# Gated linear attention and a feed-forward block on one core: reading finished sums behind all products of their tile, block sums on VectorE, and an activation of one exp and two tanh terms

## The chip, the cores and the metric

The kernel runs on 1 core of one Trainium2 chip. The metric is the device time of one execution in microseconds; lower is better. Before the change the runs shown took 700.88 us (median of 3, 696.11 to 701.51).

## The reference

Two stages follow each other. The first is a recurrent attention over 4 batches, 8 heads, 768 positions and a head size of 48; the second is a feed-forward block of 3072 tokens, model width 384 and inner width 2048.

```python
f = 1.0 / (1.0 + np.exp(-f_logit))
for t in range(S):
    state = f[:, :, t, :, None] * state + np.einsum('bhd,bhe->bhde', k[:, :, t], v[:, :, t])
    y[:, :, t] = np.einsum('bhd,bhde->bhe', q[:, :, t], state)
x = y.transpose(0, 2, 1, 3).reshape(B * S, H * D)
h = x @ w_in
sp = np.maximum(h, 0.0) + np.log1p(np.exp(-np.abs(h)))   # softplus
g = h * erf(sp)
out = g @ w_out
```

All arrays are float32.

## The kernel before, in words

**Attention** goes by chunks of 128 positions, 24 in all (`g`), in four stages each. `stage_d` (L353) multiplies the logarithms of the decays with a triangle (`ps_d`), ScalarE takes two exponentials (`dp`, `kd`, L365, L368), VectorE scales q into `qd` (L375), and GpSimd scales k into `kd` (L379; VectorE for the first three chunks). `stage_t` (L383) transposes both on TensorE and copies them out (`qT` by ScalarE, `kT` by ScalarE or, from chunk 9, by VectorE). `stage_s` (L401) makes the scores, masks them on VectorE (`A`, L421) and moves the state on: `Sn` by VectorE (L448), `Mbd` by GpSimd (L451). `stage_y` (L455) makes the output, which ScalarE copies into `xT` (L464).

**The feed-forward block** goes by blocks of 256 tokens (two chunks), 12 in all. `hidden` (L510) makes a group of 4 x 128 inner columns: 12 matmuls of 256 columns into the PSUM tile `hps`, which ScalarE (blocks 0 to 2, L527) or VectorE (blocks 3 to 11, L529) copies to SBUF as `h`. There are 48 groups. `activate` (L469) then replaces `h` by h * erf(softplus(h)), approximated: ScalarE makes e = sigmoid(h + b) (L155) and three terms x = tanh(k h + a) (L158), VectorE multiplies each into e, (x + b) * e (L163), ScalarE takes tanh(c e) (L490), VectorE multiplies with h (L493). `activate` is a generator of steps; `act_step` (L499) advances the groups in work, starts a new one when the youngest has done `LEAD` = 6 steps, and the main loop calls it at chosen slots.

**The output product** of a block is `project` (L621), a Strassen-like scheme of seven products of quarter blocks in place of eight, for which `sum_h` (L568) makes four sums of blocks of h per group (`a21 - ...`, each 128 x 256, on GpSimd, L550) and `sum_w` (L552) the sums of the weights, once, in the place `wT` where block 0's h had been. Block 0 is multiplied plainly (`project_first`, L594) for that reason. `project` holds two PSUM tiles of two banks each, out of the same pool of two as `hps`: the first, `ops[0]`, has the products 1, 2 and 6, the second, `ops[1]`, has 5, 7, 3 and 4. Two matmuls of 192 columns per product and group make 56 matmuls per block. Before the change the finished sums are read while the block's other products are still being made: product 1 is finished first and copied by ScalarE (L666), then come 2 and 6, then VectorE adds these (L658), then 5 and 7, then VectorE again, then 3 and 4, and VectorE a last time, before the block's DMA to DRAM (L589).

**The order** is written out by hand. The main loop (L836) runs 12 passes, `it`. Passes 0 to 2 make the hidden groups of blocks 0 to 3 and `project_first`; passes 3 to 10 each run `project(it - 2)` (56 slots) and then the hidden groups of block `it + 1` (48 slots); pass 11 runs the last three projects. A slot is one matmul of these generators. In the gaps between slots the loop places the attention stages of the block after next, by the list `at`, about 11 slots apart, act steps (from pass 3 at every fourth slot), steps of block sums, and `prepare` (L335), which takes Exp and Ln of a block's decays on ScalarE right behind a `stage_y`. Each engine takes its instructions strictly in the order in which this loop writes them, and a PSUM tile is handed over as a whole: an instruction that writes to a tile waits for the reads of that tile which stand ahead of it in the program. ScalarE's functions lie in tables; `use_exp_ln` (L321) loads the set with Exp and Ln, and the other functions load theirs.

The launch first rounds the weights (float64 words to float32) in `round_piece` (L272), seven VectorE operations per piece, 16 pieces; that fills VectorE until about 100 us.

Of the kernel before, what the change touches and what calls it, by code (L numbers as in the profile page):

```python
# [40 lines left out]
FP32 = mybir.dt.float32  # L42
# [9 lines left out]
SERF_C = 0.12675436  # L52
SERF_B = 0.20603738
SERF_KAB = (
    (0.50210557, -1.37006942, 1.36582221),
    (0.49818342, -0.11437819, 5.22837536),
    (0.83937711, -2.99136281, 5.68346943),
# [13 lines left out]
P = 128  # L71
# [3 lines left out]
def kernel(  # L75
# [40 lines left out]
    serf_bias = fixed("serf_bias", [P, 1 + len(SERF_KAB)])  # L116
    flag = fixed("flag", [P, 1], I32)
    for i, a in enumerate([SERF_B] + [a for _, a, _ in SERF_KAB]):
        nc.vector.memset(serf_bias[:, i : i + 1], a)
# [34 lines left out]
    def sigmoid(dst, h):  # L154
        nc.scalar.activation(out=dst[:], in_=h, func=AF.Sigmoid, bias=serf_bias[:, 0:1])  # L155

    def term(dst, h, i):
        nc.scalar.activation(  # L158
            out=dst[:], in_=h, func=AF.Tanh, bias=serf_bias[:, 1 + i : 2 + i], scale=SERF_KAB[i][0]
        )  # L160
# [171 lines left out]
    def other_set():  # L332
        sets[0] = 0
# [19 lines left out]
    def stage_d(g):  # L353
# [8 lines left out]
        use_exp_ln()  # L362
# [16 lines left out]
        (nc.vector if g < FIRST else nc.gpsimd).tensor_tensor(  # L379
# [21 lines left out]
    def stage_s(g):  # L401
# [39 lines left out]
        for r in range(2):  # L441
            total = Tall[rows(r), g, :].unsqueeze(2).broadcast_to((D, HP, D))
            if c == 0:
                nc.vector.tensor_tensor(
                    out=new[rows(r), :, r, :], in0=dS[rows(r)], in1=total, op=ALU.mult
                )
                continue
            nc.vector.tensor_tensor(  # L448
                out=Sn[rows(r)], in0=dS[rows(r)], in1=old[rows(r), :, r, :], op=ALU.add
            )  # L450
            nc.gpsimd.tensor_tensor(  # L451
                out=new[rows(r), :, r, :], in0=Sn[rows(r)], in1=total, op=ALU.mult
            )
# [15 lines left out]
    def activate(gr):  # L469
# [4 lines left out]
        other_set()  # L474
        sigmoid(e, h)
# [3 lines left out]
        for i in range(n + 2):  # L479
            if i < n:  # L480
                xs[i] = xpool.tile([P, FG * TB], FP32, name="x", tag="x")
                other_set()
                term(xs[i], h, i)
            if i >= 2:
                times(e, xs.pop(i - 2), i - 2)
            yield
        for _ in range(n):
            yield
        other_set()
        nc.scalar.activation(out=e[:], in_=e[:], func=AF.Tanh, scale=SERF_C)  # L490
        yield
# [18 lines left out]
    def hidden(blk, gi):  # L510
# [4 lines left out]
        for j in range(FG):  # L515
            ft = gi * FG + j
            assert ft * n_pieces // n_ft in rounded
            for kt in range(n_k):
# [6 lines left out]
                if j == FG - 1 and kt == n_k - 1:  # L525
                    if blk < 3:
                        nc.scalar.copy(out=gr["h"], in_=hps[:])  # L527
                    else:
                        nc.vector.tensor_copy(out=gr["h"], in_=hps[:])  # L529
                    acts.append(activate(gr))  # L530
# [18 lines left out]
    def add(out, x, y, op=ALU.add):  # L549
        nc.gpsimd.tensor_tensor(out=out, in0=x, in1=y, op=op)  # L550

    def sum_w(gi):  # L552
# [4 lines left out]
        add(t[:, 0], b12, b11, ALU.subtract)  # L557
        yield
        add(t[:, 1], b22, t[:, 0], ALU.subtract)
        yield  # L560
        add(t[:, 2], b22, b12, ALU.subtract)
        yield
        add(t[:, 3], b21, t[:, 1], ALU.subtract)
# [57 lines left out]
    def project(blk):  # L621
# [43 lines left out]
        yield from products((2, 3), (1,))  # L665
        nc.scalar.copy(out=o[:, 3, :], in_=place[1])  # L666
        yield from products((2, 3), (2, 6))

        plus(o[:, 0:5:4, :], o[:, 3:4, :].broadcast_to((P, 2, DH)), pair(2))
        yield from products((2, 3), (5, 7))  # L670

        plus(o[:, 5:7, :], o[:, 4:5, :].broadcast_to((P, 2, DH)), pair(5))
        plus(o[:, 3, :], o[:, 5, :], place[7])
        yield from products((2, 3), (3, 4))
        plus(o[:, 1:3, :], o[:, 5:7, :], pair(3))
# [41 lines left out]
    with tc.manual_schedule():  # L717
# [118 lines left out]
        for it in range(n_blocks):  # L836
            gen, n = slots(it)
            if it == 0:
                todo = [(stage_d, 3), (stage_t, 3), (stage_d, 4), (stage_s, 3), (stage_t, 4), (stage_y, 3),
                        (stage_d, 5), (stage_s, 4), (stage_t, 5), (stage_y, 4)] + stages(2)[4:]  # L840
                at = [3, 7, 11, 14, 18, 21, 36, 44, 60, 74, 78, 82, 86, 92]
# [6 lines left out]
            for s, _ in enumerate(gen):  # L848
# [26 lines left out]
                else:  # L875
                    step = s % 4 == 2
# [21 lines left out]
    def general():  # L898
# [132 lines left out]
        def second(b, r0):  # L1031
            for gi in range(n_g):
# [12 lines left out]
                sigmoid(e, h)  # L1045
# [62 lines left out]
```

## Time and profile before

| what | value |
|---|---|
| median of the runs shown | 700.88 us |
| the profiled execution's own time | 701.82 us |
| its span, first to last instruction | 700.1 us |
| TensorE busy (matmul) | 627.1 us, 90% |
| VectorE busy | 479.6 us, 69% |
| ScalarE busy | 429.0 us, 61% |
| GpSimd busy | 278.9 us, 40% |
| granted TensorE clock, mean of full speed | 0.964 |

The busy times are sums over the whole span; which engine holds up which is read from the stretches and the waits. In the rows, PE is TensorE, PEld its weight loads, DVE VectorE, ACT ScalarE, POOL GpSimd, SP the queue that issues the DMAs. A float32 matmul leaves two records, so 56 matmuls show as 112. A number behind a name such as `ops_1915` in the program's order is that of the tile, so that two tiles of one name can be told apart.

### The profile page before, as it was taken

The numbers are of one execution on the slowest core, as the hardware profiler recorded it, in microseconds if no ns is written. First come the engines' busy times: TensorE is split into PE (matmuls) and PEld (weight loads), VectorE is DVE, ScalarE is ACT, GpSimd is POOL, SyncE is SP. The second block draws the span as 40 slices with busy tenths as digits, with TensorE's granted clock in tenths as the row PEclk, the third lists the DMA queues.
The fourth block names the chain that finished last, engine by engine and source line by source line (L and its number), as shares of the span: only waits on it lengthen the run. The fifth ranks groups of instructions, "written<-read, shape, count | busy, mean of one in ns | idle before, by whom it ended". The sixth has DMA issues, their size and how long they took to land.

```text
span 700.1 us, 11595 instructions
## 1 busy us (share of the span) xinstructions
PE 627.1 (90%) x4727; PEld 545.9 (78%) x4727; DVE 479.6 (69%) x508; ACT 429.0 (61%) x474; POOL 278.9 (40%) x253
## 2 busy tenths in 40 slices
PE   7979889999795998699899799789899999899995
PEld 6858667787485888588789688678888988789895
DVE  4799996388947676477496485656857866568751
ACT  5348358587756966838676747755686645637530
POOL 0110000123967423183183170335427560724990
PEclk9999999999898999899999899989999999999999
DMA  9998611312010301211031031030110000000000
GB/s 198 257 246 239 168 35 35 57 35 46 11 46 12 68 13 26 56 33 24 13 81 23 13 68 30 17 68 12 24 36 1 1 24 1 1 22 1 23 23 27
DMA packets 120635, 37.04 MB, mean 53 GB/s; under 512 B 112384, under 2 KB 115456, under 8 KB 120576
## 3 DMA queue, kind: packets, MB, share of 16 engines
q1 hardware_dynamic: 118496, 35.84, 22.0%
q8 instruction: 39, 0.64, 0.4%
q10 hardware_dynamic: 2080, 0.39, 0.3%
q14 instruction: 20, 0.16, 0.1%
HBM read 31.46 MB, written 4.72 MB: 52 GB/s over the span
## 4 chain that ended last, share of the span: by engine, by line
PE 64%; DVE 15%; ACT 10%; issue 4%; DMA 3%; POOL 2%; SPq 0%; ACTq 0%; DVEq 0%; POOLq 0%
PE hps L519 27%; PE ops L650 24%; PE y L149 4%; DVE e L163 3%; PE sc L407 3%; ACT x L158 2%; PE ps_d L361 2%; DVE scratch L658 2%; PE ps_t L389 1%; PE ops L605 1%; DVE A L421 1%; ACT e L155 1%; ACT L325 1%; DMA Hg<-in_moe_w_in_dram 1%; DVE Hg L308 1%
## 5 line engine op out<-in xcount | busy, mean ns | idle before, releaser
L519 PE MATMUL hps<-xT,w_in_sb 128*128 128x256 f32 x1152 | 262.8, 384 | 0.0
L519 PEld LDWEIGHTS hps<-xT,w_in_sb 128*128 128x128 f32 x1152 | 217.0, 191 | 33.6 <-issue 3.4
L163 DVE SCALAR_TENSOR_TENSOR e<-x,e 128x1024 f32<-128x1024 f32 x144 | 204.4, 1419 | 25.1 <-ACT x L158 22.3
L158 ACT ACTIVATE x<-Hg,serf_bias 128x1024 f32<-128x1024 f32 x132 | 146.8, 1136 | 0.1
L379 POOL TENSOR_TENSOR kd<-kn,kd 128x384 f32<-128x384 f32 x21 | 22.6, 1077 | 241.1 <-ACT kd L368 182.1
L650 PE MATMUL ops<-w_out_sb,Hg 128*128 128x192 f32 x352 | 78.9, 339 | 17.6 <-ACT scratch L666 13.6
L155 ACT ACTIVATE e<-Hg,serf_bias 128x1024 f32<-128x1024 f32 x44 | 50.6, 1149 | 62.9 <-DVE Hg L493 60.2
L650 PE MATMUL ops<-wT,Hg 128*128 128x192 f32 x352 | 88.6, 334 | 0.0
L650 PEld LDWEIGHTS ops<-w_out_sb,Hg 128*128 128x128 f32 x352 | 61.1, 194 | 24.9 <-ACT scratch L666 16.8
L550 POOL TENSOR_TENSOR scratch<-Hg 128x256 f32<-128x256 f32 x40 | 52.5, 1312 | 66.5 <-PE ops L650 55.2
L650 PE MATMUL ops<-wT,scratch 128*128 128x192 f32 x320 | 77.3, 334 | 0.1
L529 DVE COPY Hg<-hps 128x1024 f32<-128x1024 f32 x36 | 44.0, 1223 | 39.2 <-PE hps L519 39.0
L493 DVE TENSOR_TENSOR Hg<-Hg,e 128x1024 f32<-128x1024 f32 x44 | 64.1, 1456 | 7.6 <-ACT e L490 7.3
L650 PEld LDWEIGHTS ops<-wT,Hg 128*128 128x128 f32 x352 | 63.5, 195 | 3.3 <-issue 2.0
L650 PE MATMUL ops<-w_out_sb,scratch 128*128 128x192 f32 x160 | 42.7, 350 | 25.4 <-DVE scratch L658 25.4
L451 POOL TENSOR_TENSOR Mbd<-Sn,Tall 48x192 f32<-48x192 f32 x32 | 28.5, 892 | 86.8 <-DVE Sn L448 85.6
L658 DVE TENSOR_TENSOR scratch<-scratch,ops 128x384 f32<-128x384 f32 (+1 forms) x44 | 22.1, 502 | 56.6 <-PE ops L650 34.8
L650 PEld LDWEIGHTS ops<-wT,scratch 128*128 128x128 f32 x320 | 57.6, 195 | 0.6 <-POOL scratch L550 0.6
L490 ACT ACTIVATE e<-e 128x1024 f32<-128x1024 f32 x48 | 50.2, 1045 | 6.2 <-DVE e L163 6.2
L464 ACT COPY xT<-y 128x384 f32<-128x384 f32 x24 | 11.5, 478 | 69.3 <-PE y L149 69.3
L375 DVE TENSOR_TENSOR qd<-qn,dp 128x384 f32<-128x384 f32 x24 | 14.2, 590 | 55.4 <-ACT dp L365 55.1
L650 PEld LDWEIGHTS ops<-w_out_sb,scratch 128*128 128x128 f32 x160 | 29.3, 203 | 28.3 <-DVE scratch L658 28.3
(111 smaller groups left out, 876.9 us busy)
## 6 DMA issues: line engine op xcount, KB each, us to landing
lt<-in_f_logit_dram SPq DMA_DIRECT2D x24, 192.0 KB, 3.3
qn<-in_q_dram SPq DMA_DIRECT2D x24, 192.0 KB, 3.7
out_dram<-scratch SPq DMA_DIRECT2D x12, 384.0 KB, 2.8
kn<-in_k_dram SPq DMA_DIRECT2D x23, 192.0 KB, 3.8
vt<-in_v_dram SPq DMA_DIRECT2D x23, 192.0 KB, 2.8
w_out_sb<-in_moe_w_in_dram SPq DMA_DIRECT2D x4, 768.0 KB, 6.1
Hg<-in_moe_w_in_dram SPq DMA_DIRECT2D x4, 768.0 KB, 7.8
Hg<-in_moe_w_out_dram SPq DMA_DIRECT2D x4, 768.0 KB, 6.6
```

The lines of the kernel that those rows point to most:

```text
L149: nc.tensor.matmul(y[M * i : M * (i + 1), kt, :], lhsT=terms[n][0], rhs=terms[n][1], start=(n == 0), stop=(n == len(terms) - 1), skip_grou ...
L155: nc.scalar.activation(out=dst[:], in_=h, func=AF.Sigmoid, bias=serf_bias[:, 0:1])
L158: nc.scalar.activation(out=dst[:], in_=h, func=AF.Tanh, bias=serf_bias[:, 1 + i : 2 + i], scale=SERF_KAB[i][0])
L163: nc.vector.scalar_tensor_tensor(out=e[:], in0=x[:], scalar=SERF_KAB[i][2], in1=e[:], op0=ALU.add, op1=ALU.mult)
L451: nc.gpsimd.tensor_tensor(out=new[rows(r), :, r, :], in0=Sn[rows(r)], in1=total, op=ALU.mult)
L490: nc.scalar.activation(out=e[:], in_=e[:], func=AF.Tanh, scale=SERF_C)
L493: nc.vector.tensor_tensor(out=h, in0=h, in1=e[:], op=ALU.mult)
L519: nc.tensor.matmul(hps[:, j, :], lhsT=w_in_sb[:, kt, ft * P : (ft + 1) * P], rhs=xTs[blk][:, kt, :], start=(kt == 0), stop=(kt == n_k - 1),)
L529: nc.vector.tensor_copy(out=gr["h"], in_=hps[:])
L550: nc.gpsimd.tensor_tensor(out=out, in0=x, in1=y, op=op)
L650: nc.tensor.matmul(place[n], lhsT=x[:, j, :], rhs=y, start=(gi == 0 and j == 0 and n in first), stop=(gi == n_g - 1 and j == 1), skip_grou ...
L658: nc.vector.tensor_tensor(out=out, in0=x, in1=y, op=ALU.add)
```

## The change

Five edits, in the order of the diff below.

1. The approximation of the activation has one exp and two tanh terms in place of a sigmoid and three. Per group ScalarE does four operations (exp, two tanh, the outer tanh) in place of five, VectorE three in place of four. Exp counts as usable in whichever table set is loaded: `use_exp_ln()` is no longer called in `stage_d`, and `other_set()` no longer ahead of e.
2. `kd` (all chunks) and `Mbd` are made by VectorE.
3. All hidden groups are copied from PSUM by ScalarE.
4. The block sums of h are made by VectorE; those of the weights stay on GpSimd.
5. In `project`, products 1, 2 and 6 of the last two groups are issued together, then the copy and the first addition; products 5, 7, 3 and 4 follow together, then the other three additions.

The slots of a few attention stages in pass 0, the steps of `activate` and the slots at which the loop calls it from pass 3 on (2 and 6 of every 9) move as well. Lines of the changed kernel are up to 11 lower: L666 is L657, L658 is L649, L163 is L160, L493 is L487, L550 is L541, L519 is L513.

```diff
-SERF_C = 0.12675436
-SERF_B = 0.20603738
+SERF_C = 1.41272172
 SERF_KAB = (
-    (0.50210557, -1.37006942, 1.36582221),
-    (0.49818342, -0.11437819, 5.22837536),
-    (0.83937711, -2.99136281, 5.68346943),
+    (-0.49563134, 0.05678801, 1.02373814),
+    (0.48999436, -1.29296666, 1.39467856),
 )
...
-    def sigmoid(dst, h):
-        nc.scalar.activation(out=dst[:], in_=h, func=AF.Sigmoid, bias=serf_bias[:, 0:1])
+    def exp(dst, h):
+        nc.scalar.activation(out=dst[:], in_=h, func=AF.Exp)
...
         nc.tensor.matmul(ps, lhsT=tri[:], rhs=lts[blk][:, j, :], start=True, stop=True)
-        use_exp_ln()
...
-        (nc.vector if g < FIRST else nc.gpsimd).tensor_tensor(
+        nc.vector.tensor_tensor(
             out=kd, in0=kns[g % NQ][:].rearrange("t (h d) -> t h d", d=D), in1=kd, op=ALU.mult
...
-            nc.gpsimd.tensor_tensor(
+            nc.vector.tensor_tensor(
                 out=new[rows(r), :, r, :], in0=Sn[rows(r)], in1=total, op=ALU.mult
...
-        other_set()
-        sigmoid(e, h)
+        exp(e, h)
         yield
         n = len(SERF_KAB)
         xs = {}
-        for i in range(n + 2):
-            if i < n:
-                xs[i] = xpool.tile([P, FG * TB], FP32, name="x", tag="x")
-                other_set()
-                term(xs[i], h, i)
-            if i >= 2:
-                times(e, xs.pop(i - 2), i - 2)
+        for i in range(n):
+            xs[i] = xpool.tile([P, FG * TB], FP32, name="x", tag="x")
+            other_set()
+            term(xs[i], h, i)
             yield
-        for _ in range(n):
+        for i in range(n):
+            times(e, xs[i], i)
+            yield
+        for _ in range(3):
             yield
         other_set()
         nc.scalar.activation(out=e[:], in_=e[:], func=AF.Tanh, scale=SERF_C)
         yield
-        yield
...
                 if j == FG - 1 and kt == n_k - 1:
-                    if blk < 3:
-                        nc.scalar.copy(out=gr["h"], in_=hps[:])
-                    else:
-                        nc.vector.tensor_copy(out=gr["h"], in_=hps[:])
+                    nc.scalar.copy(out=gr["h"], in_=hps[:])
...
-    def add(out, x, y, op=ALU.add):
-        nc.gpsimd.tensor_tensor(out=out, in0=x, in1=y, op=op)
+    def add(out, x, y, op=ALU.add, engine=nc.vector):
+        engine.tensor_tensor(out=out, in0=x, in1=y, op=op)
...
-        yield from products((2, 3), (1,))
+        yield from products((2, 3), (1, 2, 6))
         nc.scalar.copy(out=o[:, 3, :], in_=place[1])
-        yield from products((2, 3), (2, 6))
 
         plus(o[:, 0:5:4, :], o[:, 3:4, :].broadcast_to((P, 2, DH)), pair(2))
-        yield from products((2, 3), (5, 7))
+        yield from products((2, 3), (5, 7, 3, 4))
 
         plus(o[:, 5:7, :], o[:, 4:5, :].broadcast_to((P, 2, DH)), pair(5))
+        plus(o[:, 1:3, :], o[:, 5:7, :], pair(3))
         plus(o[:, 3, :], o[:, 5, :], place[7])
-        yield from products((2, 3), (3, 4))
-        plus(o[:, 1:3, :], o[:, 5:7, :], pair(3))
         store(blk)
...
-                at = [3, 7, 11, 14, 18, 21, 36, 44, 60, 74, 78, 82, 86, 92]
+                at = [3, 9, 12, 15, 20, 23, 36, 44, 60, 74, 78, 82, 86, 92]
...
-                    step = s % 4 == 2
+                    step = s % 9 in (2, 6)
```

The first place at which the order moves is TensorE's queue in the second half of a project (block 2 before, block 3 in the change, both in the steady passes). Before, a wait for ScalarE stands between product 1 and products 2 and 6, and a wait for VectorE between products 5, 7 and 3, 4 of the same tiles:

```order
L650 MATMUL ops_1915<-w_out_sb_61,Hg_112 128x192 x4
L650 MATMUL ops_1915<-w_out_sb_61,Hg_112 128x192 [waits Activation_49]
L650 MATMUL ops_1915<-wT_113,scratch_114 128x192
L650 MATMUL ops_1915<-w_out_sb_61,Hg_112 128x192
...
L650 MATMUL ops_1916<-wT_113,Hg_112 128x192
L650 MATMUL ops_1916<-w_out_sb_61,scratch_114 128x192 [waits DVE_49]
L361 MATMUL ps_d_2074<-lt_1746,tri_59 128x384 [waits DMAHW1_49,PE_49,Activation_49]
L650 MATMUL ops_1916<-wT_113,Hg_112 128x192
```

In the changed kernel the same half runs through with no such wait; the wait that is left stands at the next hidden group, which takes over the first tile:

```order
L641 MATMUL ops_2208<-w_out_sb_61,Hg_110 128x192
L641 MATMUL ops_2208<-wT_111,scratch_112 128x192
L641 MATMUL ops_2209<-wT_111,scratch_112 128x192
L641 MATMUL ops_2209<-wT_111,Hg_110 128x192
...
L358 MATMUL ps_d_2374<-lt_2036,tri_59 128x384 [waits DMAHW2_49,DVE_49,Activation_49]
L641 MATMUL ops_2209<-wT_111,Hg_110 128x192
...
L641 MATMUL ops_2209<-wT_111,Hg_110 128x192
L513 MATMUL hps_2400<-xT_1975,w_in_sb_60 128x256 [waits DVE_49]
```

The two waits inside the project are gone from TensorE's queue, and the reads of the first tile now have all of products 5, 7, 3 and 4 before `hps` needs the place.

The second place is ScalarE's queue in the same half: the copy of product 1 (L666, L657) against the block's `prepare` (L342 and L343, L339 and L340). Before, the copy stands ahead of the attention output and of `prepare`:

```order
L490 ACTIVATE e_2257<-e_2257 128x1024 [waits DVE_49]
L158 ACTIVATE x_2370<-Hg_112,serf_bias_62 128x1024 [waits Activation_49]
L666 COPY scratch_114<-ops_2267 128x192 [waits DMAHW4_49,PE_49]
L464 COPY xT_2382<-y_2383 128x3x128 [waits PE_49]
L325 ACT_TABLE_LOAD
L342 ACTIVATE lt_2091<-lt_2091 128x768 [waits DMAHW3_49,DMAHW2_49,DVE_49]
L343 ACTIVATE lt_2091<-lt_2091 128x768 [waits Activation_49]
```

In the changed kernel it stands behind them and behind a second table load:

```order
L460 COPY xT_2317<-y_2318 128x3x128 [waits PE_49]
L322 ACT_TABLE_LOAD
L339 ACTIVATE lt_2036<-lt_2036 128x768 [waits DMAHW3_49,DMAHW2_49,DVE_49]
L340 ACTIVATE lt_2036<-lt_2036 128x768 [waits Activation_49]
L155 ACT_TABLE_LOAD
L155 ACTIVATE x_2356<-Hg_110,serf_bias_62 128x1024
L657 COPY scratch_112<-ops_2208 128x192 [waits DMAHW4_49,PE_49]
```

The copy has moved behind five more ScalarE instructions. Over the whole queue ScalarE's table loads go from 61 to 20.

The third place is VectorE's queue in that project of the changed kernel, where a group's four block sums (L541) now stand among the attention's and the activation's work:

```order
L417 TENSOR_TENSOR A_2250<-sc_2241,tri_59 128x1024 [waits PE_49]
L444 TENSOR_TENSOR Sn_2261<-dS_2252,Mbd1_108 48x192 [waits PE_49]
...
L447 TENSOR_TENSOR Mbd0_107<-Sn_2261,Tall_109 48x4x48 [waits DVE_49]
L541 TENSOR_TENSOR scratch_112<-Hg_110 128x256 [waits PE_49]
L541 TENSOR_TENSOR scratch_112<-scratch_112,Hg_110 128x256 [waits DVE_49]
L541 TENSOR_TENSOR scratch_112<-Hg_110,scratch_112 128x256 [waits DVE_49,PE_49]
L541 TENSOR_TENSOR Hg_110<-Hg_110 128x2x128
L160 SCALAR_TENSOR_TENSOR e_2236<-x_2267,e_2236 128x1024 [waits Activation_49]
L395 COPY kT_2298<-ps_t_2292 128x512 [waits PE_49]
```

These sums and `Mbd` were GpSimd's before, which had nothing else in this stretch; here what follows them on VectorE waits behind them.

## Rows read from the trace of the kernel before

**Rows 1.** The page, part 1: busy time of each engine, its share, its instructions.

```profile
PE 627.1 (90%) x4727; PEld 545.9 (78%) x4727; DVE 479.6 (69%) x508; ACT 429.0 (61%) x474; POOL 278.9 (40%) x253
```

**Rows 2.** Busy time by stretch: length, five engines' busy time, clock, DMA share, GB/s.

```profile
0.00:90.10 90.10, 75.81 (x720) 63.18 (x720) 75.63 (x120) 46.57 (x67) 9.99 (x19) 0.98 0.85 215
90.10:141.80 51.70, 48.65 (x404) 40.09 (x405) 32.86 (x42) 33.25 (x42) 6.01 (x6) 0.97 0.23 43
141.80:257.80 116.00, 102.39 (x727) 81.36 (x726) 85.67 (x75) 83.82 (x87) 64.67 (x54) 0.94 0.17 35
257.80:541.30 283.50, 256.56 (x1958) 227.91 (x1957) 184.55 (x180) 191.51 (x202) 117.66 (x104) 0.95 0.16 32
488.30:541.30 53.00, 49.88 (x406) 44.45 (x405) 37.81 (x36) 40.84 (x43) 25.65 (x22) 1.00 0.09 20
541.30:693.90 152.60, 143.68 (x924) 133.40 (x922) 100.40 (x94) 73.88 (x77) 80.60 (x71) 1.00 0.03 11
```

**Rows 3.** Who waited for whom on TensorE: total us, times, longest.

```profile
PE ops L650 <- DVE scratch L658: 26.4, 11, 5.8
PE ops L650 <- ACT scratch L666: 13.6, 11, 3.0
PE ops L605 <- DVE wT L493: 5.2, 1, 5.2
```

**Rows 4.** Timeline of one project, 268 to 292 us: start, length, instruction, idle before.

```profile
273.63 0.75 PE L650 MATMUL ops<-w_out_sb,Hg 128*128 128x192 f32 x2 [1.98 <-ACT scratch L666]
278.62 0.48 ACT L464 COPY xT<-y 128x384 f32<-128x384 f32 x1 [3.99 <-PE y L149]
279.12 1.28 ACT L325 ACT_TABLE_LOAD   x1
280.41 0.84 ACT L342 ACTIVATE lt<-lt 128x768 f32<-128x768 f32 x1
...
283.44 1.06 ACT L490 ACTIVATE e<-e 128x1024 f32<-128x1024 f32 x1
...
286.81 0.94 DVE L658 TENSOR_TENSOR scratch<-scratch,ops 128x384 f32<-128x384 f32 x2
287.80 1.01 PE L650 MATMUL ops<-w_out_sb,scratch 128*128 128x192 f32 x2 [5.79 <-DVE scratch L658]
```

**Rows 5.** Groups by line and shape: busy us, mean ns, idle before and what ended it.

```profile
L163 DVE SCALAR_TENSOR_TENSOR e<-x,e 128x1024 f32<-128x1024 f32 x144 | 204.4, 1419 | 25.1 <-ACT x L158 22.3
L493 DVE TENSOR_TENSOR Hg<-Hg,e 128x1024 f32<-128x1024 f32 x44 | 64.1, 1456 | 7.6 <-ACT e L490 7.3
L529 DVE COPY Hg<-hps 128x1024 f32<-128x1024 f32 x36 | 44.0, 1223 | 39.2 <-PE hps L519 39.0
...
L658 DVE TENSOR_TENSOR scratch<-scratch,ops 128x384 f32<-128x384 f32 x33 | 18.2, 551 | 56.2 <-PE ops L650 34.8 <-ACT xT L464 19.3 <-ACT x L158 1.5
...
L527 ACT COPY Hg<-hps 128x1024 f32<-128x1024 f32 x8 | 8.1, 1013 | 5.0 <-PE hps L519 4.9
...
L658 DVE TENSOR_TENSOR scratch<-scratch,ops 128x192 f32<-128x192 f32 x11 | 3.9, 354 | 0.4
```

**Rows 6.** VectorE and GpSimd by time: one operation alone, and beside a GpSimd operation.

```profile
150.97 1.21 DVE L163 SCALAR_TENSOR_TENSOR e<-x,e 128x1024 f32<-128x1024 f32 x1
...
181.44 2.03 DVE L163 SCALAR_TENSOR_TENSOR e<-x,e 128x1024 f32<-128x1024 f32 x1
...
182.35 1.98 POOL L550 TENSOR_TENSOR wT<-w_out_sb 128x384 f32<-128x384 f32 x1
```

**Rows 7.** The chain that ended last, in order of time: start, length, what.

```profile
612.52 20.72 PE hps L519 x96
...
650.55 13.28 PE ops L650 x80
...
693.81 0.55 DVE scratch L658
```

**Rows 8.** Who waited for whom on ScalarE: total us, times, longest.

```profile
ACT e L155 <- DVE Hg L493: 60.2, 26, 7.3
```

More of the change, by code (lines that the diff above doesn't have):

```diff
@@ L115 @@
     w_out_sb = fixed("w_out_sb", [P, n_ft, d_model])
-    serf_bias = fixed("serf_bias", [P, 1 + len(SERF_KAB)])
+    serf_bias = fixed("serf_bias", [P, len(SERF_KAB)])
     flag = fixed("flag", [P, 1], I32)
-    for i, a in enumerate([SERF_B] + [a for _, a, _ in SERF_KAB]):
+    for i, a in enumerate(a for _, a, _ in SERF_KAB):
         nc.vector.memset(serf_bias[:, i : i + 1], a)
@@ L152, in y_matmuls @@
                         )
-    def sigmoid(dst, h):
-        nc.scalar.activation(out=dst[:], in_=h, func=AF.Sigmoid, bias=serf_bias[:, 0:1])
+    def exp(dst, h):
+        nc.scalar.activation(out=dst[:], in_=h, func=AF.Exp)
     def term(dst, h, i):
         nc.scalar.activation(
-            out=dst[:], in_=h, func=AF.Tanh, bias=serf_bias[:, 1 + i : 2 + i], scale=SERF_KAB[i][0]
+            out=dst[:], in_=h, func=AF.Tanh, bias=serf_bias[:, i : i + 1], scale=SERF_KAB[i][0]
         )
@@ L556, in sum_w @@
         t = w_sums(gi)
-        add(t[:, 0], b12, b11, ALU.subtract)
+        add(t[:, 0], b12, b11, ALU.subtract, nc.gpsimd)
         yield
-        add(t[:, 1], b22, t[:, 0], ALU.subtract)
+        add(t[:, 1], b22, t[:, 0], ALU.subtract, nc.gpsimd)
         yield
-        add(t[:, 2], b22, b12, ALU.subtract)
+        add(t[:, 2], b22, b12, ALU.subtract, nc.gpsimd)
         yield
-        add(t[:, 3], b21, t[:, 1], ALU.subtract)
+        add(t[:, 3], b21, t[:, 1], ALU.subtract, nc.gpsimd)
     def blocks(h):
@@ L1044, in second @@
                     nc.vector.tensor_copy(out=gs[gi][:, j, :], in_=hps[:, 0:TB])
-                sigmoid(e, h)
+                exp(e, h)
                 for i in range(len(SERF_KAB)):
```

## Prediction

> **What bounds the kernel now.** Start with the busy times on the page: TensorE works in 90% of the span, VectorE in 69%, ScalarE in 61% [rows 1]. So the end is set by TensorE's work plus the time in which TensorE stands, and the question is where it stands. The busy times by stretch answer that. Between 257.8 and 541.3 us lie five like passes (4 to 8, each with one project, four hidden groups and two attention chunks); TensorE is busy 256.56 of 283.50 us there. The last of the five is the fastest, 53.00 us with 49.88 busy at clock 1.00; the mean clock of the five is 0.95 [rows 2]. A pass without waits is thus near 49.9 us of TensorE, and the mean pass takes 56.7. The view of who waited for whom names the cause: 26.4 us for VectorE's additions L658 and 13.6 us for ScalarE's copy L666, each 11 times, once per project [rows 3]. Both are reads of a PSUM tile to which TensorE goes on writing. The timeline of one project shows how: after 1.98 us for the copy, TensorE waits 5.79 us more, because VectorE's addition stands behind ScalarE's xT copy, a table load, Exp, Ln, a second load and a tanh; the product behind each wait is shown with 0.75 and 1.01 us, where 80 records back to back take 13.28 us, 0.33 per product of two records [rows 4, 7]. So a wait costs twice: the wait, and work at the lower of the two clock levels behind it.
>
> **Term 1, the passes from 257.8 us on.** With products 1, 2, 6 together and 5, 7, 3, 4 together, no matmul writes to a tile once its reads have begun; in the changed order both waits are gone from TensorE's queue. TensorE's idle time is 283.50 - 256.56 = 26.9 us in the five passes and 152.60 - 143.68 = 8.9 us from there to the last product, together 35.9. Slow clock: five passes at 49.88 would be 249.4 us busy, and they were 256.56, so 7.2 more. Sum 43.0 us, nearly all of it behind these two waits, and I take it all as gone; what is late next comes in term 5.
>
> **Term 2, 141.8 to 257.8 us** (pass 2 with the plain product of block 0, and the first project). TensorE idles 116.00 - 102.39 = 13.6 us here, and the clock of 0.94 allows up to 0.06 x 116 = 7.0 more [rows 2]. One wait is for the activation of block 0 (5.2 us for L493) [rows 3]. VectorE is slow there because GpSimd works beside it: an operation of 1.21 us alone takes 2.03 beside one of GpSimd's [rows 6], and GpSimd is busy 64.7 of the 116 us. After the change GpSimd keeps only the 16 sums of weights, at 1.98 us 32 us, and a group needs 3 x 1.21 us of VectorE in place of 4 operations at 1.42 to 1.46 [rows 5]. Each act step brings a finished group nearer, too: 10 steps in place of 12. So the group for which TensorE waited is ready earlier. Ends: 6 us if only the project's own waits and a little go, 20.6 if all. I take 14, since GpSimd's weight sums still stand beside VectorE for a third of the stretch.
>
> **Term 3, the start to 141.8 us.** VectorE rounds weights, 75.6 of the first 90.1 us [rows 2]. Added to it there: two or three kd at 0.55 and some six Mbd at the 0.35 of its smallest row [rows 5], about 4 us. Removed: slowing by GpSimd, which has 19 instructions in 9.99 us there, some ten of them arithmetic; at the 0.82 us that one cost VectorE at the most [rows 2, 6] that is up to 8. The later stretch idles 51.70 - 48.65 = 3.1. Ends: 4 us slower and 8 faster; I take 3 faster.
>
> **Term 4, the end.** Behind the last product stood one addition of 0.55 us [rows 7]; now three stand there, 0.55 + 0.55 + 0.35 [rows 5]: 0.9 us slower.
>
> **Term 5, what is late next.** The load per engine is no problem. In the pass of 53.00 us VectorE is busy 37.8 [rows 2]. Four of twelve L163 go (5.7 us), the other eight and the four L493 lose some 0.22 each with GpSimd quiet (2.7), and the four copies L529 go to ScalarE (4.9, there 4 x 1.01). Sixteen block sums of 256 columns come: no row has that shape on VectorE; 192 columns take 0.354 and 384 take 0.551, so 0.42 each, 6.7 us; two kd and four Mbd add 2.5. That makes 33.7 us of a 50 us pass [rows 5]. ScalarE gives back four L158 and most of its table loads of 1.28 us, for four copies. The queues are the danger. The copy of product 1 (L657) now stands behind the xT copy, a load, Exp, Ln, a second load and one activation. In the old timeline those run from 278.62 to 284.50 us [rows 4], 5.9 us; with the copy (0.3) and VectorE's addition (0.55) and the hand-overs the first tile is free about 6.8 us after the attention output ends. The next hidden group takes that tile 19 products (0.33 each) and one ps_d (0.65) later: 6.9 us. So it just fits, and each delay of VectorE or ScalarE there shows. The ps_d ahead of it needs Ln, 3.6 us after the same point, with 11 products (3.6 us) of cover. Both are knife-edge in six passes (3 to 8). Ends: 0, and 25 us if four microseconds are lost in each; I take 5, since the old fast pass lost 3.1 with two such waits. The other three additions have a whole hidden group as cover, 12 x 0.43 = 5.2 us [rows 7], for 1.45 us of work.
>
> A rule of the Trainium skill bears on this chain: "ScalarE: Activation LUTs", section "Table sets: the hidden batching unit", puts a table load at about 2.7 us, and another section of that page at 1283 ns. The trace agrees with the second, 1.28 us [rows 4]. By 2.7 the chain would be 2.8 us longer and six passes would lose 17 us, 664 in all.
>
> **The sum.** 701.8 (the profiled execution's own time) - 43.0 - 14 - 3 + 0.9 + 5 = 647.7. The median of the runs shown is 0.9 us below that execution, so 647.
>
> **Rivals.** *The wait moves to the next tile.* ScalarE's copy, moved behind the prepare, or a VectorE queue that is behind with block sums, holds the first tile past its cover by 4 us in each of six passes: 647 - 5 + 24 to 29, about 670. For it: the chain fits with only 0.1 us to spare, and VectorE's queue now carries waits for TensorE (the first block sum waits until group 0's products have read the place). Against it: GpSimd's slowing is gone, and fewer table loads stand in the way.
>
> *Slower than before: the hidden groups' copies starve TensorE.* They now stand in ScalarE's queue behind exp, which waits for VectorE's last multiplication two groups before: such waits were 60.2 us in all, 26 times, 7.3 at the longest [rows 8]. A hidden group of 5.2 us covers a copy of 1.0 us and 4.2 of delay. Were each of 36 copies late by the longest wait, TensorE would lose 7.3 - 4.2 = 3.1 each time, 112 us, and the time would be 647 + 112 = 759. It decides from delays over 4.2 us; the mean was 60.2 / 26 = 2.3, and VectorE is to be less behind, so I give it little.
>
> *No change.* TensorE could be held by the pace of the activation as such, and the two waits be only the place where it shows; then taking them away moves 36 us of idle time elsewhere and the time stays near 700. Against it: the fast passes (541.3 on) have clock 1.00 and hardly idle with the same work per group, and VectorE and ScalarE have a third of their time free [rows 1, 2].
>
> **How the numbers follow.** The forecast has 0.75, the moved wait 0.18, the slow rival 0.04, no change 0.03. The low end is term 1 with all of terms 2 and 3 and no new wait: 701.8 - 43.0 - 20.6 - 8 + 0.9 = 631. The high end is the moved wait, 670; with both, term 2 at 6 and term 3 against me the sum would pass 680, which I leave out. That leaves about one chance in six outside, most of it above. A measurement of this kernel tells about 1% from no change; by that, the first two cases are faster: 0.93, 0.03 and 0.04.
>
> **What would show it.** Right: no wait of TensorE for L657 or L649 inside a project; passes 4 to 8 near 50 to 51 us with clock near 1.00; block sums on VectorE near 0.42 us and L160 near 1.21; GpSimd idle after about 210 us; hidden groups waiting under 1 us for L649. Wrong: TensorE waiting several microseconds for hps at the head of the hidden groups or for ps_d (the moved wait), or before each third hidden group for ScalarE's copies (the slow rival); or a stretch 141.8 to 257.8 that is no shorter, which would make term 2 nothing.

## The result, and the profile after

The changed kernel takes 637.5 us (median of 4 runs, 637.2 to 638.0); the kernel before 699.9 (4 runs, 696.1 to 701.5). The ratio is 0.912, interval 0.908 to 0.916: faster, as forecast, 9.5 us below the 647.0 predicted and inside the range. The profiled execution has a span of 635.8 us.

The page, part 1: busy time of each engine.

```profile
PE 610.8 (96%) x4727; PEld 536.7 (84%) x4727; DVE 428.5 (67%) x651; ACT 354.2 (56%) x421; POOL 25.7 (4%) x24
```

TensorE has the same 4727 records as before, yet 16.3 us less busy time [rows 1]: with fewer waits the same work took less time. Next the busy time by stretch; the columns are those of [rows 2].

```profile
139.80:240.40 100.60, 96.93 (x726) 78.55 (x725) 75.89 (x93) 64.87 (x73) 24.60 (x16) 1.00 0.20 40
240.40:488.00 247.60, 246.39 (x1959) 220.38 (x1958) 159.65 (x247) 153.74 (x177) 0.00 (x0) 1.00 0.18 37
289.40:339.20 49.80, 49.73 (x406) 44.43 (x405) 32.80 (x51) 30.63 (x35) 0.00 (x0) 1.00 0.20 41
488.00:628.90 140.90, 140.90 (x923) 133.59 (x922) 82.83 (x135) 62.56 (x68) 0.00 (x0) 1.00 0.04 12
628.90:635.80 6.90, 0.02 (x1) 0.00 (x0) 1.37 (x3) 0.00 (x0) 0.00 (x0) 0.72 0.19 64
```

The second row is passes 4 to 8: 247.60 us in place of 283.50, with 1.2 us idle in place of 26.9 and a clock of 1.00 in place of 0.95. The fourth row, the rest up to the last product, has no idle time at all. Now who waited for whom on TensorE (total us, times, longest), the four largest:

```profile
PE ps_t L385 <- DVE Sn L444: 5.9, 4, 2.1
PE ps_d L358 <- ACT qT L391: 2.0, 1, 2.0
PE ps_d L348 <- ACT kd L364: 1.9, 2, 1.0
PE ps_d L358 <- ACT lt L340: 1.5, 1, 1.5
```

Both rows that led before, L658 with 26.4 and L666 with 13.6 [rows 3], are gone, and no wait of that size has come in their place. Between instructions that are the same in both traces (to about 0.1 us) the stretches compare so:

| stretch | before, us | after, us | gained | predicted |
|---|---|---|---|---|
| start to the ps_d of pass 2 (term 3) | 139.1 | 137.0 | 2.1 | 3 |
| from there to the start of pass 4 (term 2) | 118.7 | 103.4 | 15.3 | 14 |
| passes 4 on, to the last product (terms 1 and 5) | 436.1 | 388.5 | 47.6 | 43 - 5 = 38 |
| behind the last product (term 4) | 6.2 | 6.9 | -0.7 | -0.9 |

The sum is 64.3 us, the difference of the spans, 700.1 - 635.8.

### The profile page after: what moved, and what is told of

Read it like the earlier page. It is cut to its first block, busy times and chain, and to the rows that moved or that the text cites. A ratio compares the mean times of both kernels' runs of the same rounds, so it can differ in the third digit from the quotient of the medians.

```text
span 635.8 us, 11231 instructions
## 1 busy us (share of the span) xinstructions
PE 610.8 (96%) x4727; PEld 536.7 (84%) x4727; DVE 428.5 (67%) x651; ACT 354.2 (56%) x421; POOL 25.7 (4%) x24
## 4 chain that ended last, share of the span: by engine, by line
PE 72%; DVE 15%; ACT 7%; issue 3%; DMA 2%; SPq 0%; POOL 0%; DVEq 0%; ACTq 0%; POOLq 0%
PE hps L513 30%; PE ops L641 28%; PE y L146 5%; PE sc L403 3%; PE ps_t L385 2%; PE ps_d L358 2%; ACT x L155 2%; DVE e L160 1%; DVE A L417 1%; DVE scratch L541 1%; DMA Hg<-in_moe_w_in_dram 1%; DVE w_in_sb L296 1%; DVE Hg L305 1%; PE dS L431 1%; DVE Hg L487 1%
## 5 line engine op out<-in xcount | busy, mean ns | idle before, releaser
L513 PE MATMUL hps<-xT,w_in_sb 128*128 128x256 f32 x1152 | 263.9, 384 | 1.0 <-ACT xT L460 0.6
L513 PEld LDWEIGHTS hps<-xT,w_in_sb 128*128 128x128 f32 x1152 | 216.5, 191 | 35.7 <-issue 2.6
L160 DVE SCALAR_TENSOR_TENSOR e<-x,e 128x1024 f32<-128x1024 f32 x96 | 120.0, 1250 | 23.6 <-ACT x L155 23.5
L155 ACT ACTIVATE x<-Hg,serf_bias 128x1024 f32<-128x1024 f32 x88 | 97.7, 1142 | 0.1
L152 ACT ACTIVATE e<-Hg 128x1024 f32<-128x1024 f32 x44 | 46.5, 1058 | 70.9 <-DVE Hg L487 70.4
L641 PE MATMUL ops<-w_out_sb,Hg 128*128 128x192 f32 x352 | 74.3, 328 | 0.0
L487 DVE TENSOR_TENSOR Hg<-Hg,e 128x1024 f32<-128x1024 f32 x44 | 54.2, 1231 | 28.7 <-ACT e L485 28.6
L520 ACT COPY Hg<-hps 128x1024 f32<-128x1024 f32 x44 | 44.4, 1009 | 50.2 <-PE hps L513 49.8
L649 DVE TENSOR_TENSOR scratch<-scratch,ops 128x384 f32<-128x384 f32 (+1 forms) x44 | 21.1, 501 | 65.3 <-ACT scratch L657 56.2
L417 DVE TENSOR_TENSOR A<-sc,tri 128x1024 f32<-128x1024 f32 x24 | 29.3, 1219 | 14.8 <-PE sc L403 14.6
L146 PE MATMUL y<-A,vt 128*32 128x128 f32 x768 | 35.2, 277 | 1.3 <-ACT qT L391 1.2
L146 PEld LDWEIGHTS y<-A,vt 128*32 128x32 f32 x768 | 27.3, 109 | 8.2 <-issue 3.8
L403 PEld LDWEIGHTS sc<-qT,kT 48*128 48x128 f32 x384 | 24.1, 193 | 7.6 <-issue 6.3
```

Of the source, the lines that this page charges most:

```text
L146: nc.tensor.matmul(y[M * i : M * (i + 1), kt, :], lhsT=terms[n][0], rhs=terms[n][1], start=(n == 0), stop=(n == len(terms) - 1), skip_grou ...
L152: nc.scalar.activation(out=dst[:], in_=h, func=AF.Exp)
L155: nc.scalar.activation(out=dst[:], in_=h, func=AF.Tanh, bias=serf_bias[:, i : i + 1], scale=SERF_KAB[i][0])
L160: nc.vector.scalar_tensor_tensor(out=e[:], in0=x[:], scalar=SERF_KAB[i][2], in1=e[:], op0=ALU.add, op1=ALU.mult)
L403: nc.tensor.matmul(sc[:, r, a, :], lhsT=kT[rows(r), a, :], rhs=qT[rows(r), a, :], start=True, stop=True,)
L417: nc.vector.tensor_tensor(out=A[:].rearrange("s r a t -> s (r a) t"), in0=sc[:].rearrange("s r a t -> s (r a) t"), in1=tri[:].unsqueeze(1) ...
```

## Experiments

Each ran beside the kernel before, 4 times; the ratio is to that, to be read against 0.912 (0.908 to 0.916) of the changed kernel.

| run | what | median, us | ratio (interval) |
|---|---|---|---|
| e1 | changed kernel, edit 5 undone | 684.3 | 0.979 (0.974 to 0.983) |
| e2 | kernel before with edit 5 alone | 665.7 | 0.953 (0.949 to 0.957) |
| e3 | changed, edit 4 undone | 642.0 | 0.919 (0.914 to 0.923) |
| e4 | changed, edit 1 undone | 659.6 | 0.944 (0.939 to 0.948) |
| e5 | changed, edit 3 undone | 638.3 | 0.912 (0.909 to 0.915) |
| e6 | changed, edit 2 undone | 637.5 | 0.910 (0.906 to 0.914) |
| e7 | changed, one more table load ahead of the copy | 645.4 | 0.922 (0.918 to 0.925) |
| e8 | changed, table loads of each chunk back | 645.9 | 0.922 (0.918 to 0.926) |

### e1: the reads between the products again

```diff
-        yield from products((2, 3), (1, 2, 6))
+        yield from products((2, 3), (1,))
         nc.scalar.copy(out=o[:, 3, :], in_=place[1])
+        yield from products((2, 3), (2, 6))
...
-        yield from products((2, 3), (5, 7, 3, 4))
+        yield from products((2, 3), (5, 7))
...
+        yield from products((2, 3), (3, 4))
```

> The changed kernel with the reads of the sums back between the products (edit 5 undone, all else kept). Theory A, the reads are the cause: both waits come back in each of 11 projects. With GpSimd quiet and fewer table loads each pair should cost less than the 3.6 us of before, about 1.0 us for the copy and 1.5 for the addition, 0.3 us of restart behind each, and some slow clock: 11 x 3.1 = 34 us, so 665 to 680. Rival B, the pace of the activation held TensorE and the reads only showed it: the waits stay small, 638 to 645.

Measured: 684.3, 46.8 more than the changed kernel. TensorE's waits and its busy time by stretch in e1:

```profile
PE ops L641 <- DVE scratch L649: 28.3, 11, 6.8
PE ops L641 <- ACT scratch L657: 5.8, 11, 1.4
```

```profile
243.40:520.00 276.60, 254.75 (x1957) 226.63 (x1957) 160.92 (x247) 155.03 (x177) 0.00 (x0) 0.96 0.16 33
520.00:677.70 157.70, 146.85 (x924) 136.60 (x922) 83.91 (x137) 62.57 (x68) 0.00 (x0) 0.98 0.03 11
```

The waits are back, once per project, and the cause is settled: theory A, with a size above its upper end. Per project the addition cost 28.3 / 11 = 2.6 us of waiting where 1.5 were expected, the copy 0.5 where 1.0 were. The two rows of stretches stand against the second and fourth above. Over both, e1 is 276.60 + 157.70 - 247.60 - 140.90 = 45.8 us longer; its idle time is 21.85 + 10.85 = 32.7 against 1.2, 31.5 more, and the other 14.3 us are busy time for the same products, at clock 0.96 and 0.98. Counting idle time alone would miss almost a third of what these waits cost.

### e2: the reads alone

Edit 5 as in the diff of the change, on the kernel before.

> The kernel before with the new order of products and reads alone (edit 5 alone). Theory A: the two waits, 40 us, and the slow clock behind them, 7 us, go; ScalarE's and VectorE's queues are fuller than in the changed kernel, so some of it comes back as a wait of the next hidden group for its tile, 10 to 15 us in all; 660 to 672. Rival B (pace of the activation): 690 to 702, with the idle time moved to other waits.

Measured: 665.7, 33.3 less than before, inside theory A's range. TensorE's waits in e2:

```profile
PE hps L519 <- DVE scratch L658: 6.8, 3, 4.8
PE ps_t L389 <- DVE Sn L448: 6.2, 3, 2.9
PE ops L650 <- POOL scratch L550: 5.9, 1, 5.9
PE ops L605 <- DVE wT L493: 5.2, 1, 5.2
```

The first row is the rival of the prediction in which the wait moves to the next tile: with the old, longer queues of ScalarE and VectorE the tile is not free when the hidden group wants it. Edit 5 gives 33.3 alone, the four others together 699.0 - 684.3 = 14.7 (e1), and all five 61.5. So some 13.5 us come only from having both. The 6.8 us of the first row, reads not done within the cover of the later products, would be half of that; where the rest lies isn't shown.

### e3: block sums on GpSimd again

```diff
-    def add(out, x, y, op=ALU.add, engine=nc.vector):
+    def add(out, x, y, op=ALU.add, engine=nc.gpsimd):
```

> The changed kernel with the block sums of h back on GpSimd (edit 4 undone). Theory A: VectorE has a third of its time free, so a mean L160 of about 1.4 us in place of 1.25 is covered; VectorE's busy time falls by the 75 us of the sums and rises by about 15; time within 5 us of the changed kernel, 637 to 643. Rival C, GpSimd's slowing of VectorE was what made the waits: 655 or more.

Measured: 642.0, 4.5 more by the medians and inside theory A's range; the two intervals overlap by a little. In e3's profile (of an execution of 645.2 us, 3.2 above the median) a wait of the first project for a sum is new, and the multiplications on VectorE are slower. The first fence is from the view of waits, the second from the groups by form (columns as in [rows 5]):

```profile
PE ops L641 <- POOL scratch L541: 6.6, 3, 4.3
```

```profile
L160 DVE SCALAR_TENSOR_TENSOR e<-x,e 128x1024 f32<-128x1024 f32 x96 | 132.4, 1379 | 44.3 <-ACT x L155 44.0
L541 POOL TENSOR_TENSOR Hg<-Hg 128x256 f32<-128x256 f32 x44 | 44.5, 1010 | 0.0
```

The corresponding groups of the changed kernel:

```profile
L160 DVE SCALAR_TENSOR_TENSOR e<-x,e 128x1024 f32<-128x1024 f32 x96 | 120.0, 1250 | 23.6 <-ACT x L155 23.5
L541 DVE TENSOR_TENSOR Hg<-Hg 128x256 f32<-128x256 f32 x44 | 20.0, 454 | 0.0
```

Multiplications slower by 0.13 us in the mean cost TensorE little: from one hidden group's copy to the same one a pass later, each of passes 4 to 8 is within 0.4 us of the changed kernel's. It is in the first project, where the sums of weights and of h come together on GpSimd, that e3 loses 6.4 us: TensorE waits 1.85, 0.46 and 4.26 us there, and in the 13 us around the longest wait its granted clock is 0.76.

### e4: the old activation

One sigmoid and three tanh terms, with the loads of Exp and Ln, the step order and the call slots of before; this changes the approximation back. In the diff, `exp` is the function of that name in the kernel, which now takes a sigmoid.

```diff
-    (-0.49563134, 0.05678801, 1.02373814),
-    (0.48999436, -1.29296666, 1.39467856),
+    (0.50210557, -1.37006942, 1.36582221),
+    (0.49818342, -0.11437819, 5.22837536),
+    (0.83937711, -2.99136281, 5.68346943),
...
-        nc.scalar.activation(out=dst[:], in_=h, func=AF.Exp)
+        nc.scalar.activation(out=dst[:], in_=h, func=AF.Sigmoid, bias=serf_bias[:, 0:1])
...
+        use_exp_ln()
...
+        other_set()
         exp(e, h)
...
-                    step = s % 9 in (2, 6)
+                    step = s % 4 == 2
```

> The changed kernel with the activation of before: sigmoid and three tanh terms, the act steps' old slots, and the Exp/Ln set asked for in the decay stage (edit 1 undone). Theory A: the passes keep most of their cover, the stretch of the plain product and the first project waits for block 0 and 1 again, and the chain to the first tile has more loads in it: 10 to 25 us slower, 648 to 662. Rival B: most of the 62 us gained is lost, 680 or more.

Measured: 659.6, 22.1 more, inside theory A's range. Of TensorE's waits in e4:

```profile
PE hps L518 <- DVE scratch L654: 5.4, 3, 3.4
PE ops L601 <- DVE wT L492: 4.3, 1, 4.3
```

The moved wait of e2 is here too (first row), with edits 2 to 4 in place. So without the activation's smaller share of the two queues these edits don't let the reads fit. Edits 1 and 5 without the other three were not run.

### e5 and e6: copies back on VectorE; kd and Mbd back on GpSimd

```diff
-                    nc.scalar.copy(out=gr["h"], in_=hps[:])
+                    if blk < 3:
+                        nc.scalar.copy(out=gr["h"], in_=hps[:])
+                    else:
+                        nc.vector.tensor_copy(out=gr["h"], in_=hps[:])
```

> The changed kernel, but the hidden groups of blocks 3 to 11 are copied from PSUM by VectorE again (edit 3 undone, 36 copies). Theory A (the reads behind all products carry the gain; the copy's engine is covered by the next hidden group): VectorE's load rises by about 5 us to 37 of a 49 us pass and TensorE still waits for no copy, so 636 to 642 us. Rival B (the copies had to leave VectorE, because there they stand behind multiplications and additions): each of 36 copies is late by some 0.3 us or more, 647 us or more, with waits of hps for VectorE in TensorE's list.

```diff
-        nc.vector.tensor_tensor(
+        (nc.vector if g < FIRST else nc.gpsimd).tensor_tensor(
             out=kd, in0=kns[g % NQ][:].rearrange("t (h d) -> t h d", d=D), in1=kd, op=ALU.mult
...
-            nc.vector.tensor_tensor(
+            nc.gpsimd.tensor_tensor(
                 out=new[rows(r), :, r, :], in0=Sn[rows(r)], in1=total, op=ALU.mult
```

> The changed kernel, but kd (from the fourth chunk) and Mbd are made by GpSimd again (edit 2 undone). Theory A: GpSimd works beside VectorE for some 2 x 2 + 4 x 1 us per pass and slows about that many VectorE operations, which have a third of their time free: 636 to 642 us. Rival B (this edit carries a real part of the gain, since kd feeds TensorE's transposes): waits of ps_t or of the state's products for GpSimd of over 1 us in each pass, 645 us or more.

Measured: 638.3 and 637.5, theory A in both. Neither can be told from the changed kernel. The copies, 1.22 us on VectorE (44.0 us in 36 copies) or 1.01 on ScalarE, are covered on either engine. Undone one at a time, two of the five edits move work without moving the end.

### e7: how tight the chain behind the prepare is

One table load behind Ln in passes 3 to 8 (the two that the loop writes become one):

```diff
         nc.scalar.activation(out=lt, in_=lt, func=AF.Ln, bias=1.0)
+        for _ in range(2 if blk >= 6 else 0):
+            nc.scalar.add_instruction(
+                mybir.InstLoadActFuncSet(
+                    act_func_set_id=EXP_LN, name=nc.get_next_instruction_name(),
...
```

> The changed kernel with one more table load of about 1.3 us on ScalarE behind Ln in passes 3 to 8, ahead of the copy of product 1. Theory A (the chain from the attention output to the free tile fits with nothing to spare, as the fifth term said): three or more of the six passes lose 1.0 to 1.6 us each, 3 to 9 us in all, so 641 to 647 us, with waits of hps for L649 of 1 us and more. Rival B (there is a slack of more than 1.3 us in most passes): less than 2 us in all, below 639.5 us.

Measured: 645.4, 7.9 more, inside theory A's range; six loads of 1.283 us are 7.7 us of ScalarE, an engine that is 56% busy. First the chain in the changed kernel, pass 7 (timeline, idle before in brackets), then in e7:

```profile
404.94 0.48 ACT L460 COPY xT<-y 128x384 f32<-128x384 f32 x1 [2.05 <-PE y L146]
405.43 1.28 ACT L322 ACT_TABLE_LOAD   x1
406.73 0.84 ACT L339 ACTIVATE lt<-lt 128x768 f32<-128x768 f32 x1
407.60 0.84 ACT L340 ACTIVATE lt<-lt 128x768 f32<-128x768 f32 x1
408.46 1.28 ACT L155 ACT_TABLE_LOAD   x1
409.76 1.15 ACT L155 ACTIVATE x<-Hg,serf_bias 128x1024 f32<-128x1024 f32 x1
410.81 0.30 ACT L657 COPY scratch<-ops 128x192 f32<-128x192 f32 x1
...
411.15 0.55 DVE L649 TENSOR_TENSOR scratch<-scratch,ops 128x384 f32<-128x384 f32 x1 [8.07 <-ACT scratch L657]
...
411.75 0.73 PEld L513 LDWEIGHTS hps<-xT,w_in_sb 128*128 128x128 f32 x4 [0.36 <-DVE scratch L649]
```

```profile
409.13 0.48 ACT L467 COPY xT<-y 128x384 f32<-128x384 f32 x1 [2.05 <-PE y L146]
...
416.29 0.30 ACT L664 COPY scratch<-ops 128x192 f32<-128x192 f32 x1
...
416.62 0.55 DVE L656 TENSOR_TENSOR scratch<-scratch,ops 128x384 f32<-128x384 f32 x1 [9.36 <-ACT scratch L664]
...
417.23 1.99 PE L520 MATMUL hps<-xT,w_in_sb 128*128 128x256 f32 x8 [1.35 <-DVE scratch L656]
```

In the changed kernel the hidden group starts 411.75 - 404.94 = 6.81 us after the xT copy does, 0.05 us behind the end of VectorE's addition, and its weight load stood idle for 0.36 us. In e7 it is 417.23 - 409.13 = 8.10: all of the 1.28 us shows, as a wait of 1.35. So it is in passes 4, 5 and 7 (waits of 1.26, 1.35 and 1.35). In the other three the order on ScalarE is not the one shown ahead of the prediction: in passes 3, 6 and 8 the copy L657 stands ahead of the second load. Pass 6 of the changed kernel:

```profile
359.33 0.84 ACT L340 ACTIVATE lt<-lt 128x768 f32<-128x768 f32 x1
360.08 0.30 ACT L657 COPY scratch<-ops 128x192 f32<-128x192 f32 x1
...
361.35 1.28 ACT L155 ACT_TABLE_LOAD   x1
```

Counted from the start of the xT copy, the first tile is free after 6.7 to 6.8 us in passes 4, 5 and 7, after 5.25 in passes 3 and 8 (there one activation stands between Ln and the copy) and after 4.31 in pass 6; a hidden group that nothing holds up starts after 6.58. So pass 6 has room for the load and loses nothing, and in passes 3 and 8 the tile is not late by more than 0.15 us. Yet from one hidden group's copy to the same one a pass later they are 2.4 and 3.1 us longer. The stretches behind a wait of TensorE for Sn show where, first in e7, then in the changed kernel. The row of pass 3 is the same time in both, which e7 enters 0.7 us further on in the work; the rows of pass 8 hold the same instructions:

```profile
202.60:215.00 12.40, 12.40 (x109) 11.54 (x108) 5.76 (x9) 5.49 (x7) 0.00 (x0) 0.87 0.09 18
...
478.50:496.60 18.10, 18.03 (x126) 15.46 (x127) 11.80 (x19) 8.30 (x10) 0.00 (x0) 0.91 0.00 1
```

```profile
202.60:215.00 12.40, 12.39 (x119) 11.54 (x120) 6.98 (x11) 7.17 (x10) 0.00 (x0) 1.00 0.09 18
...
471.60:488.00 16.40, 16.33 (x126) 14.23 (x127) 11.78 (x19) 8.31 (x10) 0.00 (x0) 1.00 0.00 1
```

In pass 8 the delay reached the state: the wait for Sn grew from 1.07 to 2.25 us, and behind it the clock fell and the same 126 records took 1.7 us more. In pass 3 a wait for Sn of 2.08 us, which the changed kernel has too (2.09), was followed by clock 0.87 in e7 and 1.00 there. The profiled execution of e7 is 8.6 us longer. Of these, 3.9 are theory A's, three passes with no slack at all; the rest came by the longer wait for Sn and by the clock, which neither theory had. That the load brought on the fall in pass 3 isn't shown, since the wait ahead of it was no longer.

### e8: the loads of each chunk

```diff
         nc.tensor.matmul(ps, lhsT=tri[:], rhs=lts[blk][:, j, :], start=True, stop=True)
+        use_exp_ln()
```

> The changed kernel with the Exp and Ln table set loaded again in front of the exponentials of every attention chunk, and so the other set again behind them: about two more loads of 1.28 us per chunk, some 50 us of ScalarE in all. Theory A (ScalarE has 40 percent of its time free, and only the chain behind the prepare is tight): 637 to 643 us. Rival B (the dropped loads carry the activation edit's 22 us, that is the gap of the run with the old activation): 650 to 660 us, with waits of ps_t for ScalarE's exponentials.

Measured: 645.9, between the two forecasts, so both missed; it brings 32 loads, 41 us of ScalarE. Its span is 8.5 us longer: 4.0 before pass 4, 1.2 in pass 5 (a wait of 0.72 for L650) and 3.3 in pass 8, where the wait for Sn is 2.36 and the clock 0.97, as in e7; passes 4, 6 and 7 lose nothing. If the parts add, which wasn't tried, about 8 of e4's 22 us go by table loads alone, and the other 14 belong to the dropped tanh term, its multiplication and the steps.

## Why the prediction was right, and where its terms were off

**What bounds the kernel** was read rightly: TensorE and its waits for the two reads. e1 shows it, since undoing these lines alone brings 46.8 of the 62 us back.

**Terms 1 and 5** together should have gained 38 and gained 47.6. That is nearly the whole miss (the sum gave 647.7 for the profiled execution, which took 637.6), about half in each. Term 1 had been given no margin upward: the low end of 631 came from terms 2 and 3 at their best, which is not how the time came near it. That the range held is in that part luck.

*Term 5, "I take 5", was too high.* In passes 4, 5 and 7 the chain, forecast at 6.8 us, took 6.7 to 6.8, and the hidden group started 0.15 to 0.24 us later than without it; the other knife-edge, ps_d, started right behind Ln. "It just fits" was right to a quarter of a microsecond, and then 5 us were charged for a delay that the queues did not bring: passes 4 to 8 idle 1.2 us in all. "Knife-edge in six passes" was wrong in three. The order of ScalarE's queue had been read for one block and taken for all, and in passes 3, 6 and 8 the chain has 1.3 to 2.3 us of room (e7). In the other three e7 shows that the edge is real: there TensorE lost all of 1.28 us more on ScalarE.

The page "ScalarE: Activation LUTs" of the Trainium skill, section "Table sets: the hidden batching unit", puts a load at about 2.7 us, by which we estimated 2.8 us more for a chain with two loads. The trace after does not bear this out: a load takes 1.28 us, the next instruction starts 1.30 us after the load does, twice in the chain above, and no pass lost 2.8 us.

*Term 1, 43.0, was too low by 4.6.* (The 1.2 us that passes 4 to 8 still idle are counted here; counted under term 5, the two are 5.8 and 3.8 off.) It had two faults. From 541.3 us on it took only the idle time, 8.9 us; the stretch became 152.6 - 140.9 = 11.7 us shorter. The other 2.8 us stood in the row as busy time, at a clock shown as 1.00. The timeline of TensorE before shows such a place, each product being two records:

```profile
552.42 0.49 PE L650 MATMUL ops<-wT,Hg 128*128 128x192 f32 x2
...
552.75 1.46 PE L650 MATMUL ops<-w_out_sb,Hg 128*128 128x192 f32 x8
...
554.62 0.59 PE L650 MATMUL ops<-w_out_sb,Hg 128*128 128x192 f32 x2 [0.41 <-ACT scratch L666]
...
555.05 0.49 PE L650 MATMUL ops<-wT,scratch 128*128 128x192 f32 x2
```

In a run a product is shown with 0.49 us and the next starts after 0.33, so 0.16 us of each lie beside its successor. The last product ahead of a wait has no successor beside it, and its 0.16 us count as busy time of their own; behind the wait the next product starts after 0.43, 0.10 more. That makes 0.26 us per wait beside the 0.41 shown as idle, and 2.6 of the 2.8 us for the ten waits from 541.3 us on.

The five passes hold the other fault: 49.88 us was taken for each, the busy time of a pass with 406 records. As a price for such a pass it was good; one with the same 406 records and without the two waits has 49.73 (third row of the stretches above). But the five are not alike, and [rows 2] could have told: five times 406 are 2030 records, and the five have 1958. Three of them have 382 to 391, since the first chunk of a batch has no earlier state to multiply with and the last moves none on, and take 49.0 to 49.1 us, as pass 4 here:

```profile
240.40:289.40 49.00, 49.00 (x382) 43.74 (x381) 31.17 (x49) 31.29 (x36) 0.00 (x0) 1.00 0.20 41
```

So the five take 247.6 us, not 249.4, the wait of 1.07 us for Sn in pass 8 included. These are the other 1.8 us.

**Term 2** (14, measured 15.3) and **term 3** (3, measured 2.1) held. TensorE's idle time from 139.8 to 240.4 us is 3.7, it was 13.6, and the clock rose to 1.00. The wait of 5.2 us for block 0's activation is gone. e3 shows what GpSimd's part in it was (6.4 us in that execution, if it stays in the way with the block sums), and e4, whose wait for L492 of 4.3 us is back, that the fewer steps of the activation are another part. How the 15.3 divide beyond that wasn't tried.

**Term 4** (0.9, measured 0.7): the three additions behind the last product take 1.41 us, where one took 0.55. The timeline of the end:

```profile
628.96 1.41 DVE L649 TENSOR_TENSOR scratch<-scratch,ops 128x384 f32<-128x384 f32 x3 [4.29 <-PE ops L641]
```

**The loads per engine** in term 5: VectorE was put at 33.7 us of a pass and has 32.80 in the pass of 49.80. GpSimd was forecast idle after about 210 us; it is from 194.1 on. Block sums were put at 0.42, L160 at 1.21; by line, with shortest, median and longest duration in ns:

```profile
L541 DVE TENSOR_TENSOR Hg<-Hg x44: 412/417/1235, 188.6 to 613.7; 128x256 f32<-128x256 f32 x44
```

```profile
L160 DVE SCALAR_TENSOR_TENSOR e<-x,e x96: 1201/1218/2029, 87.2 to 596.6; 128x1024 f32<-128x1024 f32 x96
```

The medians are the forecasts. The means, 0.454 and 1.250, are raised by the few long ones.

**The rivals.** *The moved wait* came in e2 (6.8 us, 3 times) and e4 (5.4, 3 times), where edit 5 meets queues of the old length, and not in the changed kernel. *The hidden copies starve TensorE*: the condition that was named for it, exp waiting for VectorE ahead of a copy, was met and even grew. On ScalarE after:

```profile
ACT e L152 <- DVE Hg L487: 70.4, 27, 7.3
...
ACT Hg L520 <- PE hps L513: 49.8, 28, 5.4
```

The first row was 60.2 before [rows 8]. But ScalarE waits for the hidden group 28 times (second row), and TensorE's list holds no wait for the copy. The timeline tells why: every exp that waited over 4.2 us, as this one of pass 6, stands under a project, between the last copy of one pass (339.27) and the first of the next (371.27), where no copy is due.

```profile
339.27 1.01 ACT L520 COPY Hg<-hps 128x1024 f32<-128x1024 f32 x1 [0.86 <-PE hps L513]
349.82 1.06 ACT L152 ACTIVATE e<-Hg 128x1024 f32<-128x1024 f32 x1 [5.74 <-DVE Hg L487]
```

The total and the longest of a wait don't say where it stands. The prediction held this rival to be unlikely because VectorE was to be less behind; these waits grew all the same, and it is their place that kept TensorE from waiting. e5 puts a number to it: on either engine these copies cost the same within 1 us. *No change*, the pace of the activation as the true bound, is refuted by e2: with the old activation at its full cost the reads alone gave 33 us.

## What to carry to other kernels

Read a finished part of an accumulator behind the last product that goes to its tile, if the work between that product and the tile's next use is longer than the chain of the read, and add that chain up instruction by instruction, for each pass by itself: here it took 6.7 to 6.8 us against 6.6 in three passes of six, where 1.28 us more showed in full, and in the other three the order of one queue left 1.3 to 2.3 us of room. A removed wait is worth more than its idle time: in e1, 31.5 us of idle time went with 14.3 us of longer products. Edits that shorten queues and edits that lengthen cover add to more than their parts (33.3 and 14.7 alone, 61.5 together), so that one of them tried by itself can look weaker than it is.

## What was not expected of the hardware

A wait of TensorE costs more than its idle time even where the granted clock is shown as 1.00: some 0.28 us for each of the ten waits from 541.3 us on in the kernel before (2.8 / 10). At the wait of 0.41 us shown above, 0.16 of it are the end of the last product ahead, with no successor beside it, and 0.10 the slower start behind it (0.59 in place of 0.49).

The clock fell behind some waits of about 2 us and not behind others: clock 0.87 behind the 2.08 us of e7 and 1.00 behind the 2.09 us of the changed kernel, at the same instruction. The fall did not come at the same point either. The first four matmuls behind the wait for Sn in pass 8 took 1.09 us in e8 (2.36 us waited) and 0.63 in the changed kernel (1.07 waited), so most of them already ran at the lower of the two levels, 1.2 GHz; in pass 3 of e7 the first four took 0.63, and only the products behind them 0.72 and 0.85 in place of 0.49. What decides between such cases stays open.

What one sum of weights costs GpSimd changes with what VectorE does beside it. Timeline of GpSimd in the changed kernel:

```profile
184.03 2.01 POOL L541 TENSOR_TENSOR wT<-w_out_sb 128x384 f32<-128x384 f32 x1
186.12 1.06 POOL L541 TENSOR_TENSOR wT<-w_out_sb,wT 128x384 f32<-128x384 f32 x1
```

From 170 to 186 us the same shape takes about 2.0 us, beside VectorE's multiplications of 1024 columns; from there it takes 1.06 to 1.20, beside VectorE's block sums of 256 columns, which are the long ones of L541 above (1.1 to 1.24 us in place of 0.42). With VectorE idle it takes 1.00 to 1.02 (e3, three sums from 187.1 us on). So VectorE's work slows GpSimd as GpSimd's slows VectorE, and the long operations cost it most. The mean over 16 is 1.57, so the estimate of 1.98 each, 32 us, was 7 too high.
